# The last output tile in two column halves, and one batch's tail sums in a later slot

## The chip, the cores and the metric

The kernel runs on one core of one Trainium2 chip. The metric is the device time of one execution in microseconds (us). TensorE is PE here, VectorE DVE, ScalarE ACT, GpSimd POOL, SyncE SP.

## What is computed

Sliding-window attention over 8 batches of 8 heads (576 positions, head size 64, window of 32 to each side), and behind it a two-layer network on the 4608 tokens of 512 features, with a smooth rectifier between the layers.

```python
def _attn_ref(q, k, v):                      # q, k, v: 8 x 8 x 576 x 64
    scores = scale * np.matmul(q, k.transpose(0, 1, 3, 2))
    mask = np.abs(pos[:, None] - pos[None, :]) <= 32
    scores = np.where(mask, scores, -1000000000.0)
...
    attn = attn / (np.sum(attn, axis=-1, keepdims=True) + 1e-09)
    return np.matmul(attn, v).astype(np.float32)

def _moe_ref(x, w_in, w_out):                # x: 4608 x 512, from the attention
    h = x @ w_in                             # w_in: 512 x 2048
    g = np.where(h >= 1, h, np.where(h <= -1, 0.0, (h + 1) ** 2 / 4))
    return (g @ w_out).astype(np.float32)    # w_out: 2048 x 512, output 4608 x 512
```

## The kernel before

The network's work is cut into 18 token tiles t of 256 tokens (`TB`), and each of these into 8 steps f of 256 hidden features. The main loop (L469) runs over "slots" a = 8 t + f, 152 of them, and writes the order of all engines out by hand: each engine runs its instructions in the order in which the loop issues them.

In a slot PE first makes the hidden part `hp` (L491): 8 matmuls of 128x256 from `xT` (the attention's output, transposed, in a ring of four batches) and `w_in`, into one of two buffers of the PSUM pool ps_h. ACT makes `rr` from it (L495), DVE a maximum `mx` (L502) and the product `gT` (L503). Before these, `flush()` issues the DVE multiplies that an earlier slot has left in the list `muls`.

Behind the hidden part, `run(a)` issues the attention steps that `at(a, ...)` has put down for this slot. Then comes the output work of a slot that lies eight behind (`post`, L472): for the first four output tiles of 128 tokens it is `pair`, from there on `quarter` (L424). A quarter is 4 of the 16 matmuls of 128x512 (L431) that make an output tile `op` in a buffer of the PSUM pool ps_o, which has two. After a tile's fourth quarter ACT copies it to `osb` (L436), and SP stores it (L437) with one DMA of 128 rows of 2 KB. Behind the output work `run(a + 0.5)` issues the steps that are put down for the half slots. The last eight slots have no hidden part left; output tile 35 (`NT // 128 - 1`), the last, takes the last four.

The attention's steps are these. `scores` makes a product of k and q in ps_s (matmuls of 64x64 tiles of PE, L227), ACT takes its exponential (L235, a 128x1024 operation) and DVE multiplies by the mask (L201); `scores8` does it for the last 96 positions of a batch. `sums` multiplies the masked exponentials by v and by ones (L293, in 64x64 tiles too) into a buffer of two banks of ps_n, which has one; its `end()` (L296) has ACT take the logarithm (L299) and the exponential of its negative (L300), and leaves the multiply into `xT` (L305, or L308 for the tail) to the next `flush()`. In `run`, all `end()`s of a half slot or slot come after all its sums and scores. A batch has five sums steps: two heads' halves (y1 = 0, 1) for each of two position ranges, and one for its tail, positions 480 to 575. `seq` lists them for batches 1 to 7 with the scores that go beside them. For batch 1, the second, the tail's sums are `seq[4][0]`.

The slots of the steps around the change (L404 to L411): sums of batch 1 at 18, 20 and 22, the last being the tail's; the first sums of batch 2 at 28 and 30; scores at 18, 20 (batch 1's tail), 26.5 (batch 2, alone there), 28, 30, and from there sums and scores together. Token tile 4, whose hidden part begins at slot 32, holds tokens 1024 to 1279: the end of batch 1, its tail among it, and the start of batch 2. Its matmuls take the four feature groups in the order 0, 2, 1, 3 (L490), so that the first two need y1 = 0 alone.

Loads come over POOL's queue; SP's queue has the stores and the transposing transfers of q and k. At the program's end (L536) SP waits in turn for the semaphores of all transfers and for the engines, and a barrier of all engines closes it.

Of the kernel before, what the change touches and what calls it, by code (L numbers as in the profile page):

```python
# [7 lines left out]
FP = mybir.dt.float32  # L8
# [6 lines left out]
def kernel(  # L15
# [19 lines left out]
    nc = tc.nc  # L35
    B, H, S, D = q.shape
    NT, DM, DFF = out.shape[0], 512, 2048
# [16 lines left out]
    osp = ctx.enter_context(tc.tile_pool(name="osp", bufs=3))  # L54
# [14 lines left out]
    w_out = const.tile([128, 16, DM], BF, name="w_out")  # L69
# [4 lines left out]
    V, P, A = nc.vector, nc.gpsimd, nc.scalar  # L74
# [296 lines left out]
    ps_o = ctx.enter_context(tc.tile_pool(name="ps_o", bufs=2, space=bass.MemoryType.PSUM))  # L371
# [5 lines left out]
    NF = DFF // 256  # L377
# [4 lines left out]
    def at(a, *todo):  # L382


        ev.setdefault(a, []).extend(x for x in todo if x)
# [15 lines left out]
    at(13.5, (*seq[1][1], ps_n))  # L401
    at(14, (*seq[0][0], ps_s), seq[1][0])
    at(16, seq[2][1])
    for n, a in enumerate((18, 20, 22, 28)):  # L404
        at(a, seq[2 + n][0])
    for n, a in enumerate((18, 20, 26.5, 28)):
        at(a, seq[3 + n][1])
# [7 lines left out]
    for b in range(LONG + 1, B):  # L415
        a = sl[5 * (b - 1) - 7] - 17
# [5 lines left out]
    gT, op = {}, {}  # L422

    def quarter(x):  # L424

        tt, ff = divmod(x, 4)
        if tt not in op:
            op[tt] = ps_o.tile([128, DM], FP, name="op", tag="op"), []
        o, done = op[tt]
        for j in range(4 * ff, 4 * ff + 4):  # L430
            nc.tensor.matmul(o, gT[tt // 2][:, j, 128 * (tt % 2):128 * (tt % 2) + 128], w_out[:, j],  # L431
                             start=not done, stop=len(done) == 2 * NF - 1, skip_group_check=True)
            done.append(j)
        if len(done) == 2 * NF:
            osb = osp.tile([128, DM], FP, name="osb")
            A.copy(osb, o)  # L436
            nc.sync.dma_start(out=out[128 * tt:128 * tt + 128, :], in_=osb)  # L437
# [31 lines left out]
    for a in range(NF * NB + NF):  # L469
# [36 lines left out]
        for x in post:  # L506
            (pair if x < 4 * 4 else quarter)(x)
# [33 lines left out]
```

The softmax here doesn't subtract the row's maximum and nothing guards it: scores larger than these inputs give would overflow.

## Time and profile before

| what | value |
|---|---|
| time, median of 4 runs | 309.56 us (309.43 to 310.02) |
| the profiled execution | 309.54 us, its span 307.8 us |
| granted TensorE clock | 0.997 |
| DVE / ACT busy | 242.4 / 192.5 us |
| last matmul's group, copy of the last tile, its issue | 302.15 to 303.84, 303.86 (0.58), 304.48 (0.33) us |
| stores: issue to landing | median 2.4 us, shortest 2.0 |

The span runs from the first to the last instruction of the profiled execution; the 1.7 us beside it lie around it. A matmul's row in the profile shows its whole length, its way through the array included (0.27 us for 256 columns, 0.38 for 512); since the next one starts before it ends, the cost of one in a series is the distance of two starts. Some matmul records are missing from the trace, so a row may show three where the kernel issues four.

### The profile page before, as it was taken

The page shows a single profiled execution, that of the slowest core. Times are in us where ns is not written, and L with a number is a line of the kernel's source. Part 1 is how long each engine was busy: PE and PEld are TensorE (multiplying, and loading weights), DVE is VectorE, ACT ScalarE, POOL GpSimd, SP SyncE. Part 2 cuts the span into 40 slices and gives each one's busy share as a digit, 9 for nine tenths or more (in the row PEclk, how much of TensorE's full clock was granted, in tenths as well). Part 3 has the DMA queues.
Part 4 walks back from the last instruction along what each step waited for, and adds up shares of the span by engine and source line. Part 5 has one row for each costly group of instructions (what it writes and reads, how often), then busy time and mean ns, then how long its engine had stood idle before and what let it go on. Part 6 is the DMA issues. An engine that isn't in the chain of part 4 may idle for free.

```text
span 307.8 us, 8422 instructions
## 1 busy us (share of the span) xinstructions
PE 294.8 (96%) x3596; PEld 205.0 (67%) x3634; DVE 242.4 (79%) x376; ACT 192.5 (63%) x319; POOL 76.8 (25%) x91
## 2 busy tenths in 40 slices
PE   8889999999999999999999999999999999999994
PEld 3567878876666666666666666666666666666651
DVE  4288568889888888889888888888888888887860
ACT  4688786747856667666656676566666666554331
POOL 8798461027009006400550002700000000000000
PEclk9999999999999999999999999999999999999998
DMA  9999999999999979996899155990911010011101
GB/s 154 185 195 197 180 201 152 166 157 164 136 188 108 190 148 105 161 89 144 108 165 138 35 108 98 149 167 8 182 44 36 34 36 36 35 36 43 62 34 68
DMA packets 137013, 35.70 MB, mean 116 GB/s; under 512 B 122128, under 2 KB 132624, under 8 KB 136976
## 3 DMA queue, kind: packets, MB, share of 16 engines
q0 software_dynamic: 102960, 18.06, 82.7%
q1 hardware_dynamic: 33872, 16.81, 24.4%
q8 instruction: 28, 0.46, 0.6%
q10 hardware_dynamic: 144, 0.29, 0.4%
q14 instruction: 9, 0.07, 0.1%
HBM read 36.70 MB, written 9.44 MB: 150 GB/s over the span
## 4 chain that ended last, share of the span: by engine, by line
PE 88%; DMA 4%; POOL 3%; issue 2%; ACT 1%; DVE 0%; POOLq 0%
PE hp L491 39%; PE op L431 35%; PE bb L293 6%; PE op L447 4%; DMA w_in<-in_moe_w_in_dram 4%; PE bb L227 2%; POOL vn L106 1%; POOL w_in L110 1%; PE tp L187 1%; ACT pt L235 1%; POOL kh L85 0%; DVE gT L500 0%; ACT mx L499 0%; PE bb L252 0%; ACT rr L495 0%
## 5 line engine op out<-in xcount | busy, mean ns | idle before, releaser
L491 PE MATMUL hp<-xT,w_in 128*128 128x256 bf16 x1152 | 149.4, 273 | 1.9 <-DMA w_in<-in_moe_w_in_dram 1.0
L495 ACT ACTIVATE rr<-hp 128x512 f32<-128x512 f32 x144 | 85.6, 594 | 88.7 <-PE hp L491 88.6
L491 PEld LDWEIGHTS <-w_in 128*128 128x128 bf16 x1152 | 112.1, 98 | 41.4 <-issue 2.7
L431 PE MATMUL op<-w_out,gT 128*128 128x512 bf16 x476 | 122.8, 379 | 5.1 <-issue 4.8
L502 DVE TENSOR_TENSOR mx<-hp,rr 128x512 f32<-128x512 f32 x137 | 94.5, 689 | 31.4 <-ACT rr L495 29.3
L503 DVE SCALAR_TENSOR_TENSOR gT<-rr,mx 128x512 bf16<-128x512 f32 x137 | 95.3, 695 | 4.7
L431 PEld LDWEIGHTS <-gT 128*128 128x128 bf16 x512 | 47.6, 98 | 36.7
L98 POOL DMA_DIRECT2D qn<-in_q_dram x12 | 14.6, 1224 | 113.0 <-DMA kT<-kn 109.2
L235 ACT ACTIVATE pt<-bb 128x1024 bf16<-128x1024 f32 (+1 forms) x33 | 32.7, 1001 | 4.3 <-PE bb L227 2.9
L305 DVE TENSOR_TENSOR xT<-bb,rc 128x512 bf16<-128x512 f32 (+1 forms) x32 | 21.0, 657 | 10.3 <-ACT rc L300 9.6
L106 POOL DMA_DIRECT2D vn<-in_v_dram x32 | 27.5, 901 | 3.4 <-DMA w_out<-in_moe_w_out_dram 3.4
L436 ACT COPY osb<-op 128x512 f32<-128x512 f32 x32 | 18.6, 582 | 11.8 <-PE op L431 11.4
L300 ACT ACTIVATE rc<-lr 128x512 f32<-128x512 f32 (+2 forms) x40 | 23.5, 587 | 1.3
L299 ACT ACTIVATE lr<-bb 128x512 f32<-128x512 f32 (+2 forms) x40 | 22.1, 552 | 0.4 <-PE bb L293 0.3
L201 DVE TENSOR_TENSOR pt<-pt,mask 128x1024 bf16<-128x1024 bf16 (+1 forms) x33 | 20.2, 613 | 0.2 <-ACT pt L235 0.2
L293 PE MATMUL bb<-pt,ones 64*64 64x256 bf16 (+3 forms) x352 | 19.6, 256 | 0.1
L293 PE MATMUL bb<-pt,vn 64*64 64x128 bf16 (+3 forms) x712 | 18.4, 204 | 0.2 <-DMA vn<-in_v_dram 0.2
L293 PEld LDWEIGHTS <-vn 64*64 64x64 bf16 x712 | 16.7, 107 | 0.4 <-DMA vn<-in_v_dram 0.4
L447 PE MATMUL op<-w_out,gT 128*128 128x256 bf16 x128 | 16.5, 273 | 0.0
L293 PEld LDWEIGHTS <-ones 64*64 64x64 bf16 x352 | 10.2, 105 | 8.6 <-issue 8.6
L98 POOL DMA_DIRECT2D kn<-in_k_dram x12 | 14.6, 1235 | 0.5 <-issue 0.5
L447 PEld LDWEIGHTS <-gT 128*128 128x128 bf16 x128 | 11.9, 98 | 1.9
(56 smaller groups left out, 107.6 us busy)
## 6 DMA issues: line engine op xcount, KB each, us to landing
out_dram<-osb SPq DMA_DIRECT2D x36, 256.0 KB, 2.4
vn<-in_v_dram POOLq DMA_DIRECT2D x32, 144.0 KB, 9.9
qn<-in_q_dram POOLq DMA_DIRECT2D x12, 288.0 KB, 6.7
kn<-in_k_dram POOLq DMA_DIRECT2D x12, 288.0 KB, 8.9
w_in<-in_moe_w_in_dram POOLq DMA_DIRECT2D x12, 128.0 KB, 6.1
w_out<-in_moe_w_out_dram POOLq DMA_DIRECT2D x3, 512.0 KB, 15.3
kh<-in_k_dram POOLq DMA_DIRECT2D x4, 144.0 KB, 5.3
qn<-in_q_dram POOLq DMA_DIRECT2D x1, 576.0 KB, 9.7
```

The costliest lines, as they stand in the source:

```text
L98: nc.gpsimd.dma_start(out=x[:, :, h], in_=src[b, NY * h:NY * h + NY].rearrange("y s d -> (y s) d") .rearrange("(u p) d -> p u d", p=128))
L106: nc.gpsimd.dma_start(out=vn[b][64 * a:64 * a + 64, :, h], in_=v[b, y:y + 2].rearrange("y s d -> (y s) d") .rearrange("(c r) d -> r c d", ...
L235: A.activation(p, ps[:, :, :w * n].rearrange(like, y=m), AF.Exp, scale=D ** -0.5)
L293: nc.tensor.matmul(bb[HD[h], a, o + c0:o + c1], ones[HD[a]] if c is None else vn[b][HD[a], c, h], p(a, h), start=n == 0, stop=True, skip_g ...
L299: A.activation(lr[:, :, :D0], bb[:, :, D0:2 * D0], AF.Ln)
L300: A.activation(rc[:, :, :D0], lr[:, :, :D0], AF.Exp, scale=-1.0)
L431: nc.tensor.matmul(o, gT[tt // 2][:, j, 128 * (tt % 2):128 * (tt % 2) + 128], w_out[:, j], start=not done, stop=len(done) == 2 * NF - 1, s ...
L447: nc.tensor.matmul(o[:, tt], gT[p][:, j, 128 * tt:128 * tt + 128], w_out[:, j, 256 * half:256 * half + 256], start=not done, stop=len(done ...
L491: nc.tensor.matmul(hp[:, j], w_in[:, kk, 256 * f + 128 * j:256 * f + 128 * j + 128], xT[:, kk, r0:r0 + TB], start=n == 0, stop=n == 3)
L495: A.activation(rr, hp, AF.Relu, scale=0.5, bias=0.5)
L502: V.tensor_max(mx, hp, rr)
L503: V.scalar_tensor_tensor(g, rr, 1.0, mx, op0=ALU.min, op1=ALU.mult)
```

## The change

Two edits. In `quarter`, the last output tile goes its own way: quarters 0 and 1 make its left 256 columns, with 16 matmuls of 128x256, quarters 2 and 3 the right ones. Each half has its own buffer of ps_o, its own copy by ACT to an `osb` of 128x256 and its own store by SP, of 128 rows of 1 KB. In the table of slots, the tail sums of batch 1 are put down for 26.5 in place of 22. There they are issued ahead of batch 2's first scores, and their `end()` comes behind these.

```diff
-    for n, a in enumerate((18, 20, 22, 28)):
+    for n, a in enumerate((18, 20, 26.5, 28)):
         at(a, seq[2 + n][0])
     for n, a in enumerate((18, 20, 26.5, 28)):
         at(a, seq[3 + n][1])
...
         tt, ff = divmod(x, 4)
+        if tt == NT // 128 - 1:
+            half, n = divmod(ff, 2)
+            if n == 0:
+                op[tt] = ps_o.tile([128, 256], FP, name="op", tag="op")
+            cols = slice(256 * half, 256 * half + 256)
+            for j in range(NF * n, NF * n + NF):
+                nc.tensor.matmul(op[tt], gT[tt // 2][:, j, 128 * (tt % 2):128 * (tt % 2) + 128], w_out[:, j, cols],
+                                 start=j == 0, stop=j == 2 * NF - 1)
+            if n:
+                osb = osp.tile([128, 256], FP, name="osb")
+                A.copy(osb, op[tt])
+                nc.sync.dma_start(out=out[128 * tt:128 * tt + 128, cols], in_=osb)
+            return
         if tt not in op:
```

## The prediction

> **What bounds the kernel now.** I read the page first, then the chain of waits, then the stretches that the change touches, instruction by instruction.
>
> ```profile
> span 307.8 us, 8422 instructions
> PE 294.8 (96%) x3596; PEld 205.0 (67%) x3634; DVE 242.4 (79%) x376; ACT 192.5 (63%) x319; POOL 76.8 (25%) x91
> ...
> PE 88%; DMA 4%; POOL 3%; issue 2%; ACT 1%; DVE 0%; POOLq 0%
> ...
> L431 PE MATMUL op<-w_out,gT 128*128 128x512 bf16 x476 | 122.8, 379 | 5.1 <-issue 4.8
> ...
> L447 PE MATMUL op<-w_out,gT 128*128 128x256 bf16 x128 | 16.5, 273 | 0.0
> ```
>
> PE is busy 96% of the span and makes 88% of the chain that ended last. Its waits are all in the first 30 us, apart from 0.16 us marked "issue" ahead of L431, 30 times. Those are missing records: 476 of 512 L431 matmuls are there, and such a group shows three instead of four. So between 30 and 304 us anything that PE needn't do comes off the end, and what ACT, DVE or a queue needn't do comes off only where PE waits for it. After the last matmul nothing is hidden: copy, store and closing are in series. The change touches one place of each sort.
>
> The first place, in the timeline of PE (start, duration, what):
>
> ```profile
> 59.75 1.04 PE L491 MATMUL hp<-xT,w_in 128*128 128x256 bf16 x8
> 60.71 0.28 PE L293 MATMUL bb<-pt,ones 64*64 64x192 bf16 x4
> ...
> 61.13 1.05 PE L447 MATMUL op<-w_out,gT 128*128 128x256 bf16 x8
> ...
> 68.11 1.03 PE L431 MATMUL op<-w_out,gT 128*128 128x512 bf16 x4
> 69.06 0.42 PE L227 MATMUL bb<-qT,kT 64*64 64x128 bf16 x16
> 69.41 1.05 PE L491 MATMUL hp<-xT,w_in 128*128 128x256 bf16 x8
> ...
> 72.13 0.29 PE L293 MATMUL bb<-pt,ones 64*64 64x224 bf16 x4
> ...
> 94.60 0.28 PE L293 MATMUL bb<-pt,ones 64*64 64x192 bf16 x4
> ...
> 94.91 0.40 PE L227 MATMUL bb<-qT,kT 64*64 64x128 bf16 x16
> ```
>
> The row at 60.71 is the tail sums of batch 1, alone behind slot 22. The one at 69.06 is the scores alone at 26.5. At 94.60 the tail sums of batch 2 and some scores run as one session, with 64*64 tiles throughout: what the change makes at 26.5.
>
> The second place, in the timeline of all engines and then in stretches of 0.25 us (the last two columns are the share of the DMA engines and GB/s):
>
> ```profile
> 303.86 0.58 ACT L436 COPY osb<-op 128x512 f32<-128x512 f32 x1 [2.87 <-PE op L431]
> 304.48 0.33 SPq L437 DMA_DIRECT2D out_dram<-osb  x1
> ```
>
> ```profile
> 66.00:66.25 0.25, 0.25 (x4) 0.23 (x3) 0.22 (x2) 0.00 (x0) 0.00 (x0) 1.00 1.10 393
> ...
> 305.25:305.50 0.25, 0.00 (x0) 0.00 (x0) 0.00 (x0) 0.00 (x0) 0.00 (x0) 1.00 0.76 287
> 305.50:305.75 0.25, 0.00 (x0) 0.00 (x0) 0.00 (x0) 0.00 (x0) 0.00 (x0) 1.00 1.01 385
> 305.75:306.00 0.25, 0.00 (x0) 0.00 (x0) 0.00 (x0) 0.00 (x0) 0.00 (x0) 1.00 0.93 352
> 306.00:306.25 0.25, 0.00 (x0) 0.00 (x0) 0.00 (x0) 0.00 (x0) 0.00 (x0) 0.66 0.09 25
> ```
>
> Copy 303.86 to 304.44, issue at 304.48, bytes from 305.30 to 306.13 by the packets' records, SP's closing wait released at 306.50, end at 307.77.
>
> **Moved sums, on PE.** In slot 22 the eight hp matmuls of 0.109 us (0.87 for 8) end their turn at 59.75 + 0.87 = 60.62, and the next step starts at 61.13: the lone session costs 0.51. Inside the joined one the same matmuls take 94.91 - 94.60 = 0.31. What falls away is one change of tile form to 64*64 and one back: **-0.20**. Everything of PE from slot 27 on is earlier by that, if nothing new makes it wait.
>
> **Moved sums, the others.** With the sums go Ln (0.49), Exp (0.52) on ACT and the multiply into xT (0.55) on DVE; no DMA goes with them, and no queue is passed. Behind the matmuls at 26.5 ACT now has the scores' exp (1.02), then Ln and Exp, and only then rr of slot 27; DVE has the mask, then the multiply, then slot 27's maximum. The two-bank tile in ps_n, which the lone session had given back long before slot 28, is now free only when that multiply ends, and slot 28's sums, the next in ps_n, wait for it. In the built order their wait counts DVE up to this multiply. When does it end? The exp, at 69.53 before, comes 0.20 earlier, at 69.33. In the joined session at 94.60 the exp starts at 95.36 and the multiply ends at 97.91, 2.55 later. So it ends at 71.88; slot 32's third hp matmul starts 0.05 behind such a multiply (79.98 to 80.03), so slot 28 is let go at 71.93. PE arrives at 72.13 - 0.20 = 71.93. The margin is nil; I take +0.00. If the chain is late, the bound is the whole gain, +0.20.
>
> What is late next: ACT's rr of slot 27 ends at about 71.8 (Exp ends 1.96 behind the exp's start in the joined session, 71.29, and rr's 0.6 overlap it a little) where it ended at 71.15, but rr of slot 28 was waiting for PE anyway (0.34 idle ahead of it) and keeps its place. DVE's maximum of slot 28 starts at about 73.1 for 72.91, behind the added 0.55, and the lag is spent by slot 28's multiply, which waits for Exp, not for DVE. Slot 32 reads xT from slot 30's multiply, and PE already waits 0.07 there (0.175 between the second and third matmul, 0.109 elsewhere). That multiply hangs on slot 30's exp, which waits for PE. So it moves with PE and the 0.07 stays.
>
> **Halves, on PE.** 16 matmuls of 512 columns become 32 of 256. L431 ran 28 of them in 6.04 us (0.216 each), 3.45 for 16; L447 and L491 run 8 of 256 in 0.87, 3.48 for 32: **+0.03**, bounds 0 to 0.05. Each half takes a buffer of ps_o: the first that of tile 33 (copied by 297.54), the second that of tile 34, copied from 300.41 to 300.99, over 1 us before it is needed.
>
> The first half's last matmul is 1.74 us (16 x 0.109) ahead of the end. Its copy and issue (0.33 on SP) run under PE's second half, on an ACT that is idle for 2.87 us there and an SP that has nothing else; its bytes are through some 1.2 us before the second half's begin (by the terms below: first byte at 302.13 + 0.38 + 0.04 + 0.83 = 303.38, last at 303.9; the second half's first byte at 305.1, both before the 0.20 is taken off). They cost nothing. Without that cover the second half would be queued behind a copy and an issue, about 0.7.
>
> **Halves, the copy.** No 128x256 copy is in the trace. ACT's rows from PSUM: 0.33 for 192 columns, 0.49 for 384, 0.585 for this copy of 512. The nearest is 192: 64 more columns at 0.8 ns give 0.38. **-0.20**; by the two rows themselves -0.25 to -0.10.
>
> **Halves, the store.** 262 KB took 0.83 us from first byte to last, at 385 GB/s in full flow. The half is 131 KB in rows of 1 KB. Rows of 1 KB went at 393 GB/s at 66.00 (the stores of L453 that a transpose had held up). 131 KB at 385 is 0.34 less: **-0.34**, bounds 0 (only latency counts) and -0.41 (half of all). Before the first byte (0.83) and behind the last (0.37) I change nothing, as an issue of 128 rows stays 128 rows.
>
> **Closing.** SP tests nine semaphores in turn at the end, 0.06 us each in its records. The last store's is the third of them; with one more store in the rotation of eight it is the fourth, so one test fewer follows: **-0.06**, bounds 0 and -0.06.
>
> **A rule against it.** L447's rows: 8 weight loads and 8 matmuls of 256 columns in 0.87, so the loads of 98 ns lie under the matmuls. The Trainium skill ("TensorE: Matmul & The Clock Gate", The mechanism) says that weight loads overlap matmuls in flight only where the row groups differ; here they never do. By it the 16 added loads would cost about 1.6 us and the sum would be +0.8. The row of this case decides. Of transfers the skill ("DMA: Bandwidth & Descriptors", Rules for kernel authors) says to coalesce small ones into large. That counts transfers; here the first half's runs under PE and only the last one's length is left over. By the rule the split would gain nothing, and the sum would be -0.43.
>
> **Sum.** -0.20 + 0.00 + 0.03 - 0.20 - 0.34 - 0.06 = -0.77. The profiled execution took 309.54 (span 307.8, 1.7 around it), the median of four is 309.56: **308.78 us** (308.77 from the one, 308.79 from the other), 0.25% faster. A measurement of this kernel can tell about 0.2% (0.62 us) from no change, that is 308.94.
>
> **Rivals.**
> - *The joined sums gain nothing:* slot 28 waits for ps_n, or slot 32 for xT, by what was saved. For it: no margin at 71.93, and the 0.07 at slot 32. Against it: the 2.55 is measured on the same work. 309.54 - 0.57 = 308.97, just within 0.2%.
> - *The last store is latency:* it lands no sooner for half the bytes. For it: 1.2 of its 2.03 us are not transfer. Against it: the bytes' 0.83 us stand between the two. 309.54 - 0.43 = 309.11; with the first rival as well 309.31.
> - *Weight loads come into the open (slower):* if the 32 loads of 98 ns stood beside 32 matmuls of 109, the last tile would take 6.62 for 3.45, +3.17 in place of +0.03: 311.9. It decides from a spacing of 0.152 us a pair on (3.45 + 0.80 + 0.62 = 4.87 over 32). Against it: 128 matmuls of L447 and 1152 of L491 at 0.109.
>
> **Chances.** The forecast 0.63 (its own range 308.5 to 308.94), the first rival 0.14, the second 0.13, both 0.05, slower 0.05. The low end is all the good bounds (-0.20 - 0.25 - 0.41 - 0.06 = -0.92, 308.62) less the 0.1 by which runs lie under the median; the high end takes in the two middle cases: 308.5 to 309.25. Faster by over 0.2%: 0.64 (rival one may just fall there), same 0.31, slower 0.05.
>
> **What would show it.** Tail sums and scores in one session 0.72 to 0.76 us long at about 68.5; slot 28's first sums matmul at about 71.93, with the multiply's end 0.05 ahead if it waits; the last 32 matmuls 0.109 apart; a last copy of 0.38; the last packets over about 0.5 us. A spacing above 0.15, a slot 28 beyond 72.1 or a store that lands 2.0 us behind its issue would prove me wrong at that step.

## The result, and the profile after

The changed kernel took 308.80 us, the median of 47 executions (308.42 to 310.17), against 309.44 for the kernel before (68 executions). The ratio is 0.9978, with a 95% interval of 0.997 to 0.9985: 0.22% faster, where 0.25% was forecast. That the time falls on the forecast of 308.78 is in part luck: the gain between these medians is 0.64 us where 0.77 was forecast, and the kernel before was 0.12 us faster here than the 309.56 that the forecast started from.

The profiled execution after took 309.31, and its span is only 0.3 us shorter than before. That difference hides the change rather than shows it, as its start was slower. The timeline of PE around the moved sums (start, duration, what):

```profile
60.22 1.04 PE L504 MATMUL hp<-xT,w_in 128*128 128x256 bf16 x8
61.09 1.04 PE L460 MATMUL op<-w_out,gT 128*128 128x256 bf16 x8
...
68.06 1.03 PE L444 MATMUL op<-w_out,gT 128*128 128x512 bf16 x4
69.01 0.28 PE L293 MATMUL bb<-pt,ones 64*64 64x192 bf16 x4
...
69.33 0.40 PE L227 MATMUL bb<-qT,kT 64*64 64x128 bf16 x16
69.66 1.05 PE L504 MATMUL hp<-xT,w_in 128*128 128x256 bf16 x8
...
72.38 0.29 PE L293 MATMUL bb<-pt,ones 64*64 64x224 bf16 x4
```

Slot 22 begins 0.47 us later than before (60.22 for 59.75), slot 27 only 0.25 later (69.66 for 69.41): 0.22 was won in between. In slot 22 the output work now follows the hidden part at once, and the joined session fills 68.93 (68.06 + 0.86) to 69.66. Slot 28's sums stand at 72.38, again 0.25 later than before, so hardly anything was lost there. The timelines of ACT (first line) and DVE show how close that was:

```profile
69.78 1.02 ACT L235 ACTIVATE pt<-bb 128x1024 bf16<-128x1024 f32 x1 [0.87 <-PE bb L227]
70.83 0.69 DVE L201 TENSOR_TENSOR pt<-pt,mask 128x1024 bf16<-128x1024 bf16 x1 [0.48 <-ACT pt L235]
71.77 0.56 DVE L308 TENSOR_TENSOR xT<-bb,rc 128x384 bf16<-128x384 f32 x1 [0.24 <-ACT rc L300]
```

The multiply into xT ends at 72.33 and slot 28's first sums matmul starts at 72.38, the 0.05 of a release by DVE: it is this multiply that lets PE go, almost at the moment when PE arrives. From the start of slot 28's last hidden-part matmul to that first sums matmul it is 0.210 us here and 0.210 to 0.215 in every other run with joined sums, always 0.05 behind the multiply. It is 0.202 or 0.203 in the profile before, in both runs of the halves alone and with the sums alone in slot 24, where the multiply is long done. So PE waits about 0.01.

The end, in the timelines of PE, ACT and SP, and then in stretches of 0.25 us (last two columns: share of the DMA engines, GB/s):

```profile
300.46 3.66 PE L433 MATMUL op<-w_out,gT 128*128 128x256 bf16 x32
300.66 0.58 ACT L449 COPY osb<-op 128x512 f32<-128x512 f32 x1 [2.87 <-PE op L444]
...
302.41 0.37 ACT L437 COPY osb<-op 128x256 f32<-128x256 f32 x1 [1.16 <-PE op L433]
302.80 2.12 SPq L438 DMA_DIRECT2D out_dram<-osb  x2
304.20 0.37 ACT L437 COPY osb<-op 128x256 f32<-128x256 f32 x1 [1.42 <-PE op L433]
```

```profile
303.75:304.00 0.25, 0.25 (x4) 0.09 (x1) 0.00 (x0) 0.00 (x0) 0.00 (x0) 1.00 0.99 340
304.00:304.25 0.25, 0.12 (x2) 0.00 (x0) 0.00 (x0) 0.05 (x1) 0.00 (x0) 1.00 0.20 62
...
305.25:305.50 0.25, 0.00 (x0) 0.00 (x0) 0.00 (x0) 0.00 (x0) 0.00 (x0) 1.00 0.21 70
305.50:305.75 0.25, 0.00 (x0) 0.00 (x0) 0.00 (x0) 0.00 (x0) 0.00 (x0) 1.00 1.00 344
305.75:306.00 0.25, 0.00 (x0) 0.00 (x0) 0.00 (x0) 0.00 (x0) 0.00 (x0) 1.00 0.35 111
```

The first half's copy lies under PE's second half, and its bytes (303.63 to 304.16 in the packets' records) are through before the second copy starts at 304.20. The last store's bytes move for 0.52 us (305.42 to 305.94 in the packets' records) where 0.83 were needed.

Since the starts differ, the profiles are read by stages below: where slot 22's first hidden-part matmul starts; from there to the copy of output tile 34 (which holds the moved sums alone); and from that copy to the end of the span (which holds the halves alone).

| us | start of slot 22 | slot 22 to copy of tile 34 | from there to the end | span |
|---|---|---|---|---|
| before | 59.746 | 240.665 | 7.355 | 307.766 |
| after | 60.217 | 240.443 | 6.852 | 307.512 |

The two stages lost 0.222 and 0.503, 0.725 together; the start gave back 0.471. The kernel before has one profile alone, but the runs below repeat its stages: 240.67 in the three profiles with the sums alone in slot 22 or 24, 7.35 to 7.37 in the four with the last tile as before. Nor is it the clock, which was 0.997 before and 1.000 after: the three profiles with 240.67 had 1.000 too.

### The profile page after: what moved, and what is told of

It reads as the page before. It is cut to its first block, busy times and chain, and to the rows that moved or that the text cites. A ratio compares the mean times of both kernels' runs of the same rounds, so it can differ in the third digit from the quotient of the medians.

```text
span 307.5 us, 8458 instructions
## 1 busy us (share of the span) xinstructions
PE 294.9 (96%) x3613; PEld 206.5 (67%) x3650; DVE 242.2 (79%) x376; ACT 192.5 (63%) x320; POOL 76.8 (25%) x91
## 4 chain that ended last, share of the span: by engine, by line
PE 88%; DMA 4%; POOL 3%; issue 2%; ACT 1%; DVE 0%; POOLq 0%; ACTq 0%
PE hp L504 39%; PE op L444 34%; PE bb L293 6%; PE op L460 4%; DMA w_in<-in_moe_w_in_dram 4%; PE bb L227 2%; PE op L433 1%; POOL vn L106 1%; POOL w_in L110 1%; PE tp L187 1%; ACT pt L235 1%; POOL kh L85 0%; DVE gT L513 0%; ACT mx L512 0%; PE bb L252 0%
## 5 line engine op out<-in xcount | busy, mean ns | idle before, releaser
L504 PE MATMUL hp<-xT,w_in 128*128 128x256 bf16 x1152 | 149.3, 273 | 2.3 <-DVE gT L513 1.0
L504 PEld LDWEIGHTS <-w_in 128*128 128x128 bf16 x1152 | 112.1, 98 | 41.7 <-issue 2.1
L444 PE MATMUL op<-w_out,gT 128*128 128x512 bf16 x461 | 119.6, 379 | 5.0 <-issue 4.8
L444 PEld LDWEIGHTS <-gT 128*128 128x128 bf16 x496 | 46.1, 98 | 34.8
L300 ACT ACTIVATE rc<-lr 128x512 f32<-128x512 f32 (+2 forms) x40 | 23.5, 587 | 1.3
L299 ACT ACTIVATE lr<-bb 128x512 f32<-128x512 f32 (+2 forms) x40 | 22.1, 552 | 0.6 <-PE bb L293 0.5
L460 PE MATMUL op<-w_out,gT 128*128 128x256 bf16 x128 | 16.5, 273 | 0.0
L460 PEld LDWEIGHTS <-gT 128*128 128x128 bf16 x128 | 12.0, 98 | 1.9
```

Source lines behind the costliest of these rows:

```text
L299: A.activation(lr[:, :, :D0], bb[:, :, D0:2 * D0], AF.Ln)
L300: A.activation(rc[:, :, :D0], lr[:, :, :D0], AF.Exp, scale=-1.0)
L460: nc.tensor.matmul(o[:, tt], gT[p][:, j, 128 * tt:128 * tt + 128], w_out[:, j, 256 * half:256 * half + 256], start=not done, stop=len(done ...
L504: nc.tensor.matmul(hp[:, j], w_in[:, kk, 256 * f + 128 * j:256 * f + 128 * j + 128], xT[:, kk, r0:r0 + TB], start=n == 0, stop=n == 3)
```

## The experiments

Each was built from the kernel before or after and ran beside the kernel before on the same chip.

**The sums alone.** The kernel before with the table of slots of the changed one.

```diff
-    for n, a in enumerate((18, 20, 22, 28)):
+    for n, a in enumerate((18, 20, 26.5, 28)):
```

> Only the tail sums of batch 1 moved from slot 22 to 26.5; the last tile as before. My theory (joining two sessions saves one change of tile form each way, and the rest of the chip keeps up): from slot 22's first hidden-part matmul to the copy of tile 34, 240.66 us before, 240.45; the time 0.20 to 0.22 us shorter, ratio 0.9993. Rival (nothing gained, slot 28 or slot 32 waits by what was saved): that stretch stays 240.66, with slot 28's first sums matmul a bare 0.05 behind the end of a multiply into xT. The end, 7.36 us from tile 34's copy to the end of the span, unchanged for both.

Measured: slot 22 to tile 34's copy 240.45, from there 7.36. The time could not tell: ratio 0.9992 (0.998 to 1.0004). Once more, with the expectation

> Only the moved sums again. My theory: stages 240.45 and 7.36 again, ratio 0.9993 within its interval. Rival (no gain): 240.66, ratio 1.0.

the stages were 240.45 and 7.36 again, the ratio 1.0001 (0.9989 to 1.0013). So the stage shows the 0.21 twice, to the hundredth, and 11 or 12 executions of the whole kernel don't resolve it: the times of one such set spread from 308.96 to 310.40.

**The halves alone.** The new branch of `quarter`, with the tail sums back in slot 22.

```diff
-    for n, a in enumerate((18, 20, 26.5, 28)):
+    for n, a in enumerate((18, 20, 22, 28)):
         at(a, seq[2 + n][0])
```

> Only the last tile in two halves; the tail sums stay in slot 22. My theory: from tile 34's copy to the end of the span 6.81 us in place of 7.36 (PE +0.04, a second wait ahead of the last copy +0.04, the copy -0.21, the store -0.30, closing -0.06 to -0.12), the time 0.5 to 0.55 us shorter, ratio 0.9983; from slot 22 to tile 34's copy 240.66 as before. Rival (the gain of both comes from the sums, and the store is latency alone): 7.1 or more, ratio 0.9991.

Measured: 240.67 and 6.85, ratio 0.9994 (0.998 to 1.0008), an interval that held both theories. The 6.85 is 0.04 over what was expected, since the closing gave 0.06 and not the 0.12 that the 6.81 counted on. Again:

> Only the halves again, beside the two below on the same chip, as its first ratio (0.9994, interval 0.998 to 1.0008) held both theories. My theory (the 0.51 us of the end are in the trace, and the start before slot 22, between 59.4 and 60.4 us, hid them in few runs): stages 240.66 and 6.85 again, ratio 0.9983 within its interval. Rival (the halves cost something ahead of slot 22): slot 22 above 60.2 again and a ratio of 0.999 or more.

Measured: slot 22 at 59.50, stages 240.67 and 6.85, ratio 0.9983 (0.9974 to 0.9992). That speaks against the rival: the first time slot 22 began at 60.38, this time at 59.50, with the same edit.

**Later, but alone.** Is it the joining, or would any later slot do?

```diff
-    for n, a in enumerate((18, 20, 22, 28)):
+    for n, a in enumerate((18, 20, 24, 28)):
```

> The tail sums in a later slot too, 24, but alone there as they were in 22; the last tile as before. My theory (the gain is the joining, not the slot): from slot 22 to tile 34's copy 240.66 as before, within 0.03, and a lone session of 0.5 us behind slot 24's hidden part; the time the same. Rival (a later slot itself relieves ACT and DVE, and with them PE): 240.45, 0.2 us shorter.

Measured: 240.67 and 7.37, ratio 1.0003 (0.9989 to 1.0017). PE's timeline has the lone session in its new place:

```profile
62.91 1.04 PE L491 MATMUL hp<-xT,w_in 128*128 128x256 bf16 x8
63.88 0.28 PE L293 MATMUL bb<-pt,ones 64*64 64x192 bf16 x4
...
64.52 0.81 PE L431 MATMUL op<-w_out,gT 128*128 128x512 bf16 x3 [0.16 <-issue]
65.17 1.04 PE L491 MATMUL hp<-xT,w_in 128*128 128x256 bf16 x8
```

The hidden part's turn ends at 63.78, and the quarter begins at 65.17 - 4 x 0.216 = 64.31 (its first record is missing): 0.53 for the lone session, as in slot 22. Lateness is worth nothing; the joining is.

**Too late.** How near is the edge at slot 28?

```diff
-    for n, a in enumerate((18, 20, 22, 28)):
+    for n, a in enumerate((18, 20, 27.5, 28)):
```

> The tail sums alone at 27.5, so near to slot 28 that their multiply into xT can't be done when slot 28's sums want the buffer. My theory: Ln 0.49, Exp 0.52 and the multiply 0.55 with 0.15 of hops make 1.7 us behind the sums' last matmul, less the 1.0 that PE has to do in between (0.15 of change of tile form, 0.87 of slot 28's hidden part): PE waits 0.6 to 0.8 us ahead of slot 28's first sums matmul, released by DVE's multiply, and from slot 22 to tile 34's copy it is 241.3 to 241.5 with the session left alone. The time 0.6 to 0.9 us longer than before. Rival (the buffer of the sums is no matter): 240.66.

Measured: 241.55 and 7.35, ratio 1.0038 (1.0024 to 1.0051). PE's timeline, and DVE's:

```profile
71.41 0.28 PE L293 MATMUL bb<-pt,ones 64*64 64x192 bf16 x4
...
71.83 1.05 PE L491 MATMUL hp<-xT,w_in 128*128 128x256 bf16 x8
73.69 0.29 PE L293 MATMUL bb<-pt,ones 64*64 64x224 bf16 x4 [0.82 <-DVE xT L308]
```

```profile
73.08 0.56 DVE L308 TENSOR_TENSOR xT<-bb,rc 128x384 bf16<-128x384 f32 x1 [0.31 <-ACT rc L300]
```

PE stood 0.82 us ahead of slot 28's sums until the multiply (73.08 + 0.56 = 73.64) gave the buffer of ps_n back, 0.05 later. That is the first rival of the prediction, made to happen by moving the sums one slot further. The wait is 0.02 over the range expected of it, and the stage 0.05. The time is 1.2 us longer by the ratio (0.7 to 1.6), over the 0.6 to 0.9 expected; the stages account for 0.89 of it.

**The changed kernel again.**

> The changed kernel again, beside the three below on the same chip. My theory: slot 22 to tile 34's copy 240.44, from there to the end of the span 6.85, as in its first profile, whatever the start of the run does (slot 22 reached between 59.4 and 60.5 us); the time 0.6 to 0.8 us under before. Rival (the end or the middle scatters too): these two move by 0.1 or more.

Measured: 240.45 and 6.86, slot 22 at 60.32; ratio 0.998 (0.9966 to 0.9994). The stages repeat within 0.01.

**Halves, one store.** The last tile's two halves are copied apart and stored together.

```diff
-                osb = osp.tile([128, 256], FP, name="osb")
-                A.copy(osb, op[tt])
-                nc.sync.dma_start(out=out[128 * tt:128 * tt + 128, cols], in_=osb)
+                if half == 0:
+                    op["osb"] = osp.tile([128, DM], FP, name="osb")
+                A.copy(op["osb"][:, cols], op[tt])
+                if half:
+                    nc.sync.dma_start(out=out[128 * tt:128 * tt + 128, :], in_=op["osb"])
```

> Both edits, but the two halves of the last tile are copied into one buffer of 128x512 and stored by one DMA of 256 KB after the second copy. It tells the store's share from the copy's. My theory (the bytes of the last store are on the path): issue to release 2.03 us as before the change, tile 34's copy to the end 6.85 + 0.31 + 0.06 (the store is again third of nine in the closing) - 0.04 (the last copy waits for PE alone) = 7.18. Rival (a store is latency): 6.85 to 6.9.

Measured: 240.45 and 7.18; issue to release 2.02 us, as before the change, for 1.73 with two stores. SP's waits at the end of this kernel, and of the changed one:

```profile
SPq L551 <- DMA out_dram<-osb: 1.5, 1, 1.5
```

```profile
SPq L549 <- DMA out_dram<-osb: 1.2, 1, 1.2
```

The last store's bytes are on the path: the second rival falls. The ratio was 0.9984 (0.9972 to 0.9997).

**A buffer for each half.** In the changed kernel ACT waits ahead of the last copy in two instructions: the first for PE and an old store, the second, the copy itself, for an earlier copy of ACT's own. The chain that ended last shows the first as `ACTq` and the way from it to the copy as issue (start, duration):

```profile
304.13 0.03 ACTq L437
304.16 0.04 issue
304.20 0.37 ACT osb L437
```

The likely reason for the second wait is that the tile takes a buffer of the pool that an earlier copy has filled; which rule of the build asks for it wasn't looked into.

```diff
-                osb = osp.tile([128, 256], FP, name="osb")
+                osb = const.tile([128, 256], FP, name=f"osb{half}")
```

> Both edits, but each half of the last tile has an osb buffer of its own, so that the last copy waits for PE alone. In the changed kernel it waits for two things in two instructions: 0.081 us from the end of the last matmul to the copy, where other copies take 0.037. My theory: from tile 34's copy to the last copy 3.49 us for 3.537, to the end 6.81 for 6.85. Rival (the 0.04 is PE's): 3.537 stays.

Measured: from tile 34's copy to the last copy 3.493 for 3.537, to the end 6.825 for 6.852 (the closing took 0.02 more); ratio 0.9969 (0.9958 to 0.998). The last copy now waits in one instruction and starts 0.037 behind the last matmul for 0.081: the 0.044 was the split wait.

**The place in the closing.** With that, the stores of tiles 30 to 34 are cut in two.

```diff
             A.copy(osb, o)
-            nc.sync.dma_start(out=out[128 * tt:128 * tt + 128, :], in_=osb)
+            for c in range(0, DM, 256 if tt >= NT // 128 - 6 else DM):
+                w = 256 if tt >= NT // 128 - 6 else DM
+                nc.sync.dma_start(out=out[128 * tt:128 * tt + 128, c:c + w], in_=osb[:, c:c + w])
```

> As the one before, and the stores of output tiles 30 to 34 are each cut into two column halves, so that five more transfers go round the rotation of eight semaphores and the last store's is the last of the nine that are tested in the closing, not the fourth. No other work is changed. My theory: five tests of 0.06 us fewer behind the last landing: from the release to the end 0.89 us for 1.19, from tile 34's copy to the end 6.51. Rival (the closing is a fixed length, or the added stores hold up the last one): 6.81 or more.

Measured: release to end 0.887 us for 1.191 in the changed kernel and 1.209 with a buffer for each half, tile 34's copy to the end 6.49; median 308.42, ratio 0.9954 (0.9941 to 0.9968). Again:

> Both edits with a buffer for each half and five more transfers in the rotation, again, as only five of its executions counted. My theory: stages 240.44 and 6.49 again, which is 1.09 us under before: ratio 0.9965. Rival (its first ratio, 0.9954, was right by more than the stages): 0.995 or less, with a stage shorter.

Measured: stages 240.45 and 6.49, median 308.16, ratio 0.9958 (0.9945 to 0.997). By its stages this kernel is faster than both: they are 1.08 us under those of the kernel before, where the change has 0.73. Each set has five executions, and both ratios lie somewhat under the 0.9965 of the stages, which both intervals just hold; whether its starts were shorter by chance stays open.

## Why the prediction was right, step by step

| step | forecast | measured in the profiles |
|---|---|---|
| joining the sums (PE) | -0.20 | -0.22 (before and after), -0.21 (sums alone), the next row's 0.01 included |
| wait of slot 28 for ps_n | 0.00, at most +0.20 | about 0.01 |
| slot 32's wait for xT | stays 0.07 | 0.175 between its second and third matmul, as before |
| 32 matmuls for 16 | +0.03 | +0.04 (0.1092 apart; tile 34's copy to the last 3.493 with a buffer for each half, for 3.453) |
| (not forecast) second wait ahead of the last copy | 0 | +0.04 |
| the copy | -0.20 | -0.21 (372 ns for 585) |
| the store | -0.34 | -0.30 (issue to release 1.726 for 2.026) |
| closing | -0.06 | -0.07 |
| sum | -0.77 | -0.72 by the rows, -0.725 by the stages; -0.64 between the medians |

**Joining.** Right, with its reason: the same sums in a later slot of their own gain nothing, and joined to a session they gain 0.21. Where the form stays 128*128 a change of operation costs nothing: from L504 to L460 in the rows above it is 0.87 (60.22 to 61.09), eight times 0.109. The Trainium skill ("TensorEngine Tiling (Array Packing)", Key Properties) says that changing the tiling mode drains TensorE, without a price; this case gives one, about 0.2 us for the change to 64*64 and back. The trace doesn't show the drain itself, nor how much of the 0.2 it is.

**The margin at slot 28.** The forecast put the multiply's release and PE's arrival on the same hundredth, 71.93. Shifted by the 0.47 of the later start, that is 72.40; PE came at 72.37 and was let go at 72.38. It rested on a duration of the same work elsewhere in the trace (2.55 us from the exp's start to the multiply's end); here it was 72.33 - 69.78, 2.55 again. That the wait stayed at 0.01 is in part luck all the same: with no margin, a chain longer by 0.05 would have cost 0.05.

**The store.** The mechanism was right, and the size a little off. I took the bytes' time as 131 KB less at 385 GB/s. The packets' records show 47 ns for a piece of 1 KB and 86 for one of 2 KB, where half of 86 would be 43. With eight pieces for each of the 16 DMA engines, 0.14 is left beside them in both stores (0.83 = 8 x 0.086 + 0.14, 0.52 = 8 x 0.047 + 0.14). So 0.31 was saved, not 0.34. The 393 GB/s that the prediction read for rows of 1 KB at 66.00 didn't carry over: the last store flowed at 344. Why it was slower than those stores isn't shown.

**The last copy.** The forecast let it start like any other copy behind its last matmul, 0.037 us after. It started 0.081 after, for its wait was split over two instructions. This is the one term of any size that was missing; a buffer for each half took it away.

**Weight loads in the open.** The slower rival asked for a spacing of 0.152 us a pair. It was 0.109. The sentence of the Trainium skill ("TensorE: Matmul & The Clock Gate", The mechanism) that weight loads overlap matmuls in flight only where the row groups differ doesn't hold for these 32 pairs of 128x128 weights, though the same section also names a background weight buffer for which a load is pulled ahead, and that fits the rows.

**Between the medians.** The medians differ by 0.64 where the stages lost 0.73; the interval of the ratio, 0.15% to 0.30% or 0.46 to 0.93 us, holds both. The start is what blurs it. From slot 10 to slot 22 every profile here took 27.36 to 27.38 us, but slot 4 begins between 22.1 and 23.5 and slot 22 between 59.4 and 60.4. PE's waits of the first 45 us, of the changed kernel's second profile (slot 22 at 60.32) and of the one with buffers of their own (59.38):

```profile
PE hp L504 <- DMA w_in<-in_moe_w_in_dram: 1.7, 2, 1.1
```

```profile
PE hp L504 <- DMA w_in<-in_moe_w_in_dram: 1.1, 2, 0.7
```

In these two the loads of `w_in` land later and sooner, and what PE loses there is kept: 0.6 of the 0.94 between their slots 22. It isn't these loads alone: in the first profile after, PE waits 0.9 for `w_in` and 1.0 for DVE's `gT` in the same stretch. The start's scatter of 1 us is larger than the whole change. What decides in which order these loads land was not tried.

## What to carry to other kernels

Where one engine is busy all the time, a gain is what that engine needs not do: here a change of tile form saved by putting two 64x64 sessions together, which can be read off a place in the same trace where they are already joined. Behind the last matmul everything is in series, so the last tile's copy and store are worth cutting as long as the work of the second piece hides the copy and store of the first (two halves were tried here, not more). And where the start of a kernel scatters by more than an edit is worth, compare stages between two fixed instructions: here they repeated to about 0.01 us, where the times of a dozen executions couldn't tell the joined sums from nothing.

## What the runs showed of the hardware

- SP's closing tests are on the path: 0.06 us for each semaphore that stands behind the last store's in the row. Five places further back in the rotation took 0.30 us off (release to end 1.191 to 0.887; 0.32 against the 1.209 with a buffer for each half), for stores that cost nothing where they were cut.
- A wait that is split over two instructions cost 0.044 us on ACT (the copy 0.081 behind the last matmul for 0.037), though what the second asked for was long done.
- A store of 128 rows took 1.71 to 1.73 us from issue to release with rows of 1 KB and 2.02 to 2.04 with rows of 2 KB; with bytes moving for 0.52 and 0.83, 1.2 us of either are not bytes.
